# Attention and two dense layers on one core: the last batch passes layer one whole, and the weight conversion is divided anew

## The chip, the cores and the metric

The kernel runs on one core of a Trainium2 chip. The metric is the device time of one launch in microseconds (us). Engines are named as the profile names them: PE (matrix engine; PEld is its weight load), DVE (vector), ACT (scalar), POOL (GpSimd) and SP (the queue that issues all DMAs here).

## What is computed

Attention over 4 batches x 8 heads, 576 positions, head size 64, in which only scores within `tau` of the row's maximum count; then two dense layers over the 4 x 576 = 2304 tokens, each of width 512 with 2048 hidden units.

```python
scores = scale * (q @ k.T)
scores = where(scores >= max(scores) - tau, scores, -1e9)
attn = softmax(scores);  x = attn @ v
h = x @ w_in1;  g = where(h >= 1, h, where(h <= -1, 0, (h + 1)**2 / 4));  x = g @ w_out1
h = x @ w_in2;  g = h * clip(h + 3, 0, 6) / 6;                            out = g @ w_out2
```

The dense weights come as 64-bit numbers. Every product is made of three passes over split operands (high part x high, high x low, low x high).

## The kernel before

**Tokens.** The first 512 positions of a batch are a wide group; the last 64 of all four batches make one more group of 256 (the tail group). DRAM buffers `xd`, `x2p`, `x2d` hold the input of layer one, a partial output and the output of layer one, one buffer for each of the five groups.

**Hidden units** go in 16 blocks of 128, `f` = 0 to 15. A block of a group is `em_h` (line 520: 12 matmuls into a bank of PSUM, then the activation on DVE, ACT and DVE, lines 538 to 540, the split into `gh` on ACT, line 546, and `gl` on POOL, line 547), and later its share of the output (`em_part`, line 575, for narrow groups, `em_out`, line 556, for wide ones: 12 matmuls in all).

**Weights.** `split_a` and `split_b` (lines 107 and 129) turn one item (half of a block's weights, 128 x 512) into a high and a low part: ACT line 114, DVE lines 116, 119 (on POOL while the attention runs alone), 121 and 123, POOL line 125, ACT line 131, POOL line 133. There are 64 items, 32 for each layer. `Weights.half()` emits half an item; the callbacks `ahead1`, `ahead2`, `ahead3` say how many go ahead of each block. The loaded raw item lies in one of two buffers `w_raw`. Blocks 0 to 8 have fixed space (`wbase`), which layer two takes over when layer one has used it for the last time.

**Stages.** (1) Attention alone, with 18 items converted beside it. (2) From the first finished batch on, `dense1` (line 644) feeds narrow groups (256 tokens, 9 blocks of hidden units) of layer one into the attention: nine groups, the last of them the tail group; what is left of them runs behind the attention. Their sums go to `x2p`. (3) `dense` (line 668) takes the five wide groups through the other 7 blocks, reads `x2p` back (`load_part`), adds it (`fin_whole`, line 609) and stores `x2d`. (4) `dense` again: layer two, 16 blocks of each group, `fin_out`.

**Space.** The narrow groups' tiles lie in a pool `mt`. At the end of stage 2 it is closed and two pools, `mt2` and `g2` with the wide groups' `r`, `gh` and `gl`, are opened in the same place (lines 769 to 772), so their first writers wait for the last readers of `mt`, the stores to `x2p`.

**Order.** A scheduler of the framework places the instructions by its own plan of times within the dependencies; each engine then runs its list in that order. Every block's last ACT, DVE and POOL instruction is a pin (line 550) behind which the next conversion item is put.

Of the kernel before, what the change touches and what calls it, by code (L numbers as in the profile page):

```python
# [18 lines left out]
def kernel(  # L19
# [12 lines left out]
    nc = tc.nc  # L32
# [10 lines left out]
    NG = NT // GRP  # L43
# [3 lines left out]
    NF1 = 9  # L47
    NE = 1
# [4 lines left out]
    CSTEP = 2  # L53

# [34 lines left out]
    def load_w(kind, m, f):  # L89
        t = stage.tile([128, 512, 2], U32, tag="w_raw", name="w_raw", bufs=2)  # L90
# [48 lines left out]
    class Weights:  # L139
# [11 lines left out]
        def prefetch(self):  # L151
            while self.loaded < min(len(self.items), self.done + 2):
# [96 lines left out]
    def unit_qk(j, nm, h):  # L249
# [15 lines left out]
        else:  # L265
# [5 lines left out]
            T.transpose(tm[:, MAIN:SEQ], n[0:TAIL, 4, :], ident[0:TAIL, 0:TAIL])  # L271
# [224 lines left out]
    xsp = {"p": mt, "x": mt, "g": None, "bufs": 1, "xt": "io"}  # L496
    H_TAGS = ["Q2"]
    A_TAGS = ["P0", "P1"]

    def split_x(key):  # L500
        m, g, ph = key
        n = GRP if ph == 1 else WIDE[g]
        src = narrow(xd, g) if ph == 1 else (x2d if m == 1 else xd)[g]
        r = []
        for kk in range(KD):
            if kk % 2 == 0:
                t = xsp["x"].tile([128, 2, n], F32, tag=xsp["xt"], name="xst", bufs=2)
# [12 lines left out]
    def em_h(key, m, f):  # L520
# [14 lines left out]
        hp_, hb = (mt, HOLD) if key[2] == 1 else (xsp["g"], MLAG + 1)  # L535
# [108 lines left out]
    def dense1(ready, ahead):  # L644

        for n, l in enumerate(steps):
            if n < n_h:
                g, f = divmod(n, NF1)
                key = (0, g, 1)
                if key not in xs:  # L650
                    while not ready(g):
                        yield None
                    split_x(key)
                ahead(n, f)
                yield from em_h(key, 0, f)
                if f == NF1 - 1:
                    xs.pop(key)
                    if g + 1 < NG and ready(g + 1):
                        split_x((0, g + 1, 1))
                    if g + 1 == NG:  # L660
                        xsp.update(x=ctx.enter_context(tc.tile_pool(name="xs2", bufs=1)), xt="xst", bufs=2)
                        split_x((0, 0, 2))
                yield 0.33
# [4 lines left out]
    def dense(m, ph, groups, fs, fin, ahead, following):  # L668

        seq = [(g, f) for g in groups for f in fs]  # L670
        splits = [(m, g, ph) for g in groups] + following

        def out_block(n, i):
            g, f = seq[n]
            em_out((m, g, ph), m, f, f == fs[0], f == fs[-1], fin, i)
# [3 lines left out]
        for n, (g, f) in enumerate(seq):  # L679
# [3 lines left out]
            ahead(n, f)  # L683
            for c in em_h(key, m, f):
                pass
            if f == fs[-3] and m == 0:
                load_part(g)
            if f == fs[-2]:
                for nxt in splits[splits.index(key) + 1:][:1]:
                    split_x(nxt)  # L690
            if f == fs[-1]:
# [71 lines left out]
    wpool["p"] = ctx.enter_context(tc.tile_pool(name="wext", bufs=1))  # L763
# [4 lines left out]
    H_TAGS[:] = ["Q0", "Q1", "Q2", "Q3"]  # L768
    mt_es.close()
    xsp["p"] = ctx.enter_context(tc.tile_pool(name="mt2", bufs=1, side="right"))  # L770
    xsp["g"] = ctx.enter_context(tc.tile_pool(name="g2", bufs=1, side="right"))
    wpool["e"] = ctx.enter_context(tc.tile_pool(name="wmore", bufs=1, side="right"))

    def ahead2(n, f):
        k = n - (NW - 1) * len(fs2) - MLAG - 1
# [3 lines left out]
        if n < len(fs2):  # L779
            weights.upto(2 * KF - 2 * len(fs2) + 2 * n + 2)  # L780

    def ahead3(n, f):
# [36 lines left out]
```

## Time and profile before

| | us |
|---|---|
| median of 3 runs (lowest, highest) | 1255.71 (1251.21, 1258.08) |
| the profiled execution | 1253.57 |
| its span, first to last instruction | 1251.8 |
| PE busy | 1179.3 (94%) |
| DVE busy | 776.8 (62%) |
| POOL busy | 749.3 (60%) |
| ACT busy | 647.0 (52%) |

The shares are means over stages that differ. Matmuls overlap in the records (one of 512 columns is recorded with 0.39 us, the next begins earlier), so how fast PE works is read from the starts of matmuls, and how much it loses from its idle time and from the granted clock of a stretch.

### The profile page before, as it was taken

The page shows a single profiled execution, that of the slowest core. Times are in us where ns is not written, and L with a number is a line of the kernel's source. Part 1 is how long each engine was busy: PE and PEld are TensorE (multiplying, and loading weights), DVE is VectorE, ACT ScalarE, POOL GpSimd, SP SyncE. Part 2 cuts the span into 40 slices and gives each one's busy share as a digit, 9 for nine tenths or more (in the row PEclk, how much of TensorE's full clock was granted, in tenths as well). Part 3 has the DMA queues.
Part 4 walks back from the last instruction along what each step waited for, and adds up shares of the span by engine and source line. Part 5 has one row for each costly group of instructions (what it writes and reads, how often), then busy time and mean ns, then how long its engine had stood idle before and what let it go on. Part 6 is the DMA issues. An engine that isn't in the chain of part 4 may idle for free.

```text
span 1251.8 us, 19651 instructions
## 1 busy us (share of the span) xinstructions
PE 1179.3 (94%) x6964; PEld 1005.2 (80%) x6964; DVE 776.8 (62%) x1620; ACT 647.0 (52%) x1201; POOL 749.3 (60%) x749
## 2 busy tenths in 40 slices
PE   7889999899999999989998889998999999999998
PEld 5555579888988989989997677896888888888886
DVE  6988888888888888697728888468721121121111
ACT  5766667778787888665414344343432222232222
POOL 6999768889998999766616665336722222222221
PEclk9999999999999999989999899999999999999999
DMA  5444431122222211153313444334100010000000
GB/s 137 120 117 116 115 85 49 53 66 58 66 67 58 75 49 38 46 181 123 119 42 114 152 122 152 118 115 121 51 18 34 1 37 31 1 35 1 17 1 34
DMA packets 100881, 91.81 MB, mean 73 GB/s; under 512 B 51376, under 2 KB 85168, under 8 KB 100784
## 3 DMA queue, kind: packets, MB, share of 16 engines
q1 hardware_dynamic: 100784, 90.57, 24.4%
q8 instruction: 55, 0.90, 0.3%
q14 instruction: 42, 0.34, 0.1%
HBM read 71.66 MB, written 18.87 MB: 72 GB/s over the span
## 4 chain that ended last, share of the span: by engine, by line
PE 57%; DVE 16%; POOL 15%; issue 5%; DMA 3%; ACT 2%; SPq 1%; POOLq 0%; DVEq 0%; ACTq 0%
PE Q L529 22%; PE P L571 19%; PE Q L586 5%; POOL Gl L373 4%; PE P L311 3%; DVE w_c L116 2%; PE Q L348 2%; DVE p L327 2%; DVE w_c L119 2%; PE Q L403 2%; PE Q L401 2%; DVE w_c L121 2%; DMA w_raw<-in_moe_w_in_dram 2%; POOL Gh L374 2%; POOL w_c L119 2%
## 5 line engine op out<-in xcount | busy, mean ns | idle before, releaser
L547 POOL TENSOR_TENSOR gl<-r,gh 128x256 fp32r<-128x256 f32 (+1 forms) x196 | 207.8, 1061 | 366.5 <-ACT gh L546 327.6
L529 PE MATMUL Q<-xh,wih 128*128 128x256 f32 (+1 forms) x784 | 267.6, 343 | 10.0 <-DVE r L540 9.2
L529 PE MATMUL Q<-xl,wih 128*128 128x256 f32 (+1 forms) x784 | 264.3, 337 | 4.5 <-DVE xl L512 4.4
L529 PE MATMUL Q<-xh,wil 128*128 128x256 f32 (+1 forms) x784 | 263.5, 337 | 0.0
L543 DVE SCALAR_TENSOR_TENSOR r<-r,Q 128x512 f32<-128x512 f32 (+1 forms) x80 | 50.6, 634 | 265.3 <-ACT r L542 263.0
L529 PEld LDWEIGHTS Q<-xh,wih 128*128 128x128 f32 x784 | 150.2, 192 | 29.5 <-DVE r L540 11.3
L529 PEld LDWEIGHTS Q<-xl,wih 128*128 128x128 f32 x784 | 150.7, 192 | 20.6 <-DVE xl L512 5.3
L546 ACT ACTIVATE gh<-r 128x256 fp32r<-128x256 f32 (+1 forms) x196 | 100.9, 515 | 122.4 <-DVE r L543 45.4
L529 PEld LDWEIGHTS Q<-xh,wil 128*128 128x128 f32 x784 | 150.7, 192 | 14.9
L327 DVE SCALAR_TENSOR_TENSOR p<-p,th,e 128x576 f32<-128x576 f32 x144 | 149.4, 1041 | 13.6 <-ACT e L323 10.5
L373 POOL TENSOR_TENSOR Gl<-pf,Gh 128x512 fp32r<-128x512 f32 (+1 forms) x110 | 147.1, 1337 | 15.7 <-ACT Gh L372 10.3
L542 ACT ACTIVATE r<-Q,three 128x512 f32<-128x512 f32 (+1 forms) x80 | 51.5, 644 | 165.8 <-PE Q L529 161.3
L323 ACT ACTIVATE e<-p,nm 128x576 f32<-128x576 f32 x144 | 111.0, 771 | 34.0 <-DVE p L322 32.8
L539 ACT ACTIVATE r<-r,half 128x256 f32<-128x256 f32 (+1 forms) x116 | 64.2, 557 | 117.5 <-DVE r L538 117.3
L125 POOL TENSOR_TENSOR w_c<-w_c,w_raw 128x512 int32<-128x512 int32 x64 | 90.0, 1407 | 57.1 <-DVE w_c L123 36.4
L571 PE MATMUL P<-woh,gh 128*128 128x512 f32 x288 | 113.3, 395 | 6.0 <-DVE ob L611 3.3
L322 DVE TENSOR_SCALAR_CACHE_REDUCE p<-P 128x576 f32<-128x576 f32 x144 | 107.4, 747 | 18.0 <-PE P L298 10.6
L311 PE MATMUL P<-kst,qh 128*128 128x288 f32 x320 | 99.5, 326 | 16.3 <-DVE xu L444 6.3
L571 PE MATMUL P<-wol,gh 128*128 128x512 f32 x288 | 113.2, 393 | 0.0
L571 PE MATMUL P<-woh,gl 128*128 128x512 f32 x288 | 111.9, 393 | 0.0
L586 PE MATMUL Q<-gh,woh 128*128 128x256 f32 x324 | 97.3, 300 | 0.7 <-DVE ob L597 0.5
L586 PE MATMUL Q<-gl,woh 128*128 128x256 f32 x324 | 92.5, 285 | 1.2 <-POOL gl L547 1.1
(102 smaller groups left out, 2739.9 us busy)
## 6 DMA issues: line engine op xcount, KB each, us to landing
w_raw<-in_moe_w_in_dram SPq DMA_DIRECT2D x32, 512.0 KB, 3.9
w_raw<-in_moe_w_out_dram SPq DMA_DIRECT2D x32, 512.0 KB, 3.7
qn<-in_q_dram SPq DMA_DIRECT2D x32, 256.0 KB, 3.6
xst<-xd SPq DMA_DIRECT2D x20, 256.0 KB, 3.2
x2p<-ob SPq DMA_DIRECT2D x18, 256.0 KB, 2.4
kn<-in_k_dram SPq DMA_DIRECT2D x32, 128.0 KB, 2.2
xd<-xu SPq DMA_DIRECT2D x16, 256.0 KB, 2.3
xst<-xd SPq DMA_DIRECT2D x8, 512.0 KB, 3.9
```

The costliest lines, as they stand in the source:

```text
L125: x = G.tensor_tensor(out=c.bitcast(I32), in0=c.bitcast(I32), in1=r, op=ALU.add)
L311: mm = T.matmul(s[:, e, 0:HS], l, r[:, e * HS:(e + 1) * HS], start=(x == 0), stop=(x == len(ops) - 1))
L322: V.tensor_scalar(out=p, in0=s, scalar1=-1.0, scalar2=3e38, op0=ALU.mult, op1=ALU.min, accum_out=nm)
L323: S.activation(out=e, in_=p, func=ACTF.Exp, bias=nm, scale=-1.0)
L327: V.scalar_tensor_tensor(out=p, in0=p, scalar=th, in1=e, op0=ALU.is_le, op1=ALU.mult, accum_out=zt[j][:, i:i + 1])
L373: G.tensor_tensor(out=lo[:, :, d], in0=f[:, 0:4, b], in1=f32(hi[:, 0:4, d]), op=ALU.subtract)
L529: mm = T.matmul(h, l[:, kk * 128:(kk + 1) * 128], r, start=(x == 0), stop=(x == 3 * KD - 1))
L539: S.activation(out=r, in_=r, func=ACTF.Square, scale=0.5, bias=half)
L546: x = S.activation(out=gh, in_=r, func=ACTF.Copy)
L547: y = G.tensor_tensor(out=gl, in0=r, in1=f32(gh), op=ALU.subtract)
L571: T.matmul(a, l, r, start=(first and x == 0), stop=(last and x == 2))
L586: mm = T.matmul(o, l, r, start=(f == 0 and x == 0 and i == 0), stop=(f == NF1 - 1 and x == 2 and i == 1), skip_group_check=True)
```

## The change

- **Narrow groups** cover batches 0, 1 and 2 alone (six groups instead of nine), with ten blocks of hidden units instead of nine. Twenty items of weights are converted before and beside the attention instead of eighteen.
- **Batch 3 and the tail group** pass layer one in one piece behind the narrow groups, all 16 blocks, without `x2p`; batches 0 to 2 follow with the 6 blocks that are left. Layer two's order is batch 3, 0, 1, the tail, batch 2.
- **The switch.** A pool `g1` of its own holds the wide groups' tiles for the first four wide blocks; the second halves of the last narrow group's sums (`behind`) are emitted behind those blocks' first matmuls; `mt` is closed after them.
- **Layer two's weights** wait for the tail group to use a block for the last time (`n_free`), so their conversion begins some blocks into the tail group; a third `w_raw` buffer is added.
- **The conversion behind the attention**: the sign bit is taken off by ACT (`Abs`) instead of DVE; line 119's clamp stays on DVE. During the attention the mask is on DVE and the clamp on POOL, now also beside hosted blocks.
- `split_x` loads a wide group in four pieces through three buffers instead of two pieces through two. Sums that need no `x2p` go out by ACT and DVE in turn. A transpose of 64 rows of K becomes one of 128.

```diff
-    NG = NT // GRP
+    NG = (NB - 1) * MAIN // GRP
-    NF1 = 9
-    NE = 1
+    NF1 = 10
+    RAW = 3
...
-        x = V.tensor_scalar(
-            out=c, in0=t[:, :, 1], scalar1=0x7FFFFFFF, scalar2=None, op0=ALU.bitwise_and)
-        after(x, pins["V"])
-        (V if mode["mlp"] else G).tensor_scalar(
-            out=f32(c), in0=f32(c), scalar1=2.0 ** -15, scalar2=122879.9921875, op0=ALU.max, op1=ALU.min)
+        if mode["att"]:
+            x = V.tensor_scalar(
+                out=c, in0=t[:, :, 1], scalar1=0x7FFFFFFF, scalar2=None, op0=ALU.bitwise_and)
+            G.tensor_scalar(
+                out=f32(c), in0=f32(c), scalar1=122879.9921875, scalar2=2.0 ** -15, op0=ALU.min, op1=ALU.max)
+        else:
+            S.activation(out=f32(c), in_=f32(t[:, :, 1]), func=ACTF.Abs)
+            x = V.tensor_scalar(
+                out=f32(c), in0=f32(c), scalar1=2.0 ** -15, scalar2=122879.9921875, op0=ALU.max, op1=ALU.min)
+            after(x, pins["V"])
...
-            T.transpose(tm[:, MAIN:SEQ], n[0:TAIL, 4, :], ident[0:TAIL, 0:TAIL])
+            T.transpose(tm[:, MAIN:MAIN + 128], n[:, 4, :], ident)
...
+                src = pool.tile([128, n], F32, tag="xst", name="xst", bufs=3)
+                nc.sync.dma_start(out=src, in_=(x2d if m == 1 else xd)[g][:, kk, :])
...
+            if n == n_h - 3 and not mode["att"]:
+                split_x((0, NB - 1, 2))
...
+    def behind():
+        for l in steps[n_h:]:
+            for g, half, f in l:
+                for _ in em_part((0, g, 1), half, f):
+                    pass
+                yield
...
+    NLATE = 2
+    early = ctx.enter_context(tc.tile_pool(name="wext", bufs=1))
+    for f in range(NF1, KF - NLATE):
+        wpool[f] = early
+    wide["x"] = ctx.enter_context(tc.tile_pool(name="xs2", bufs=1))
+    g_es = ExitStack()
+    wide["g"] = g_es.enter_context(tc.tile_pool(name="g1", bufs=1))
...
+    seq2 = [(g, f) for g in (NB - 1, NB) for f in range(KF)]
+    n_free = len(seq2) - KF + MLAG + 1
+    seq2 += [(g, f) for g in range(NB - 1) for f in fs2]
+    n_last = len(seq2) - len(fs2) + MLAG + 1
+    left = behind()
+    SWITCH = MLAG + 2
+    def rest(n):
+        if n <= MLAG:
+            for _ in range(100 if n == MLAG else 4):
+                if next(left, 0) == 0:
+                    break
+        if n == MLAG:
+            H_TAGS[:] = ["Q0", "Q1", "Q2", "Q3"]
+            mt_es.close()
+            wide["p"] = ctx.enter_context(tc.tile_pool(name="mt2", bufs=1, side="right"))
+            wide["g2"] = ctx.enter_context(tc.tile_pool(name="g2", bufs=1, side="right"))
+    def ahead2(n, g, f):
...
+        limit = 2 * KF if n > SWITCH + MLAG else 2 * (KF - NLATE)
+        limit += 2 * max(0, min(n - n_free, NF1)) + 2 * max(0, n - n_last)
         for _ in range(2):
-            if weights.done < 2 * KF + 2 * NF1 + 2 * NE + max(0, 2 * (k - NE)):
+            if weights.done < limit:
                 weights.half()
...
-    order2, order3 = list(range(NW)), list(range(NW - 2)) + [NW - 1, NW - 2]
+    order3 = [NB - 1, *range(NB - 2), NB, NB - 2]
```

**DVE just behind the attention.** `xl` is the low part of a split input (128x512 of a wide group, 128x256 of a narrow one or the tail), `w_c` a weight item in conversion, `r` a block's activation. Before:

```order
L116 TENSOR_SCALAR w_c_7568<-w_raw_7469 128x512
L119 TENSOR_SCALAR w_c_7568<-w_c_7568 128x512
L121 TENSOR_SCALAR w_c_7568<-w_c_7568 128x512
L538 TENSOR_SCALAR r_7588<-Q1_7575 128x256
L123 SCALAR_TENSOR_TENSOR w_c_7568<-w_raw_7469,w_c_7568 128x512
L512 TENSOR_TENSOR xl_8906<-xst_8903,xh_8905 128x512
L512 TENSOR_TENSOR xl_8910<-xst_8903,xh_8909 128x512
L540 TENSOR_TENSOR r_7588<-Q1_7575,r_7588 128x256
L512 TENSOR_TENSOR xl_8916<-xst_8913,xh_8915 128x512
L538 TENSOR_SCALAR r_7625<-Q2_7612 128x256
```

Now:

```order
L125 TENSOR_SCALAR w_c_7572<-w_c_7572 128x512
L522 TENSOR_TENSOR xl_7984<-xst_7981,xh_7983 128x512
L128 TENSOR_SCALAR w_c_7572<-w_c_7572 128x512
L548 TENSOR_SCALAR r_7592<-Q1_7579 128x256
L130 SCALAR_TENSOR_TENSOR w_c_7572<-w_raw_7487,w_c_7572 128x512
L522 TENSOR_TENSOR xl_7990<-xst_7987,xh_7989 128x512
L522 TENSOR_TENSOR xl_7640<-xst_7637,xh_7639 128x256
L522 TENSOR_TENSOR xl_7996<-xst_7993,xh_7995 128x512
L548 TENSOR_SCALAR r_7629<-Q2_7616 128x256
L522 TENSOR_TENSOR xl_7644<-xst_7637,xh_7643 128x256
```

The mask has gone from the item's head; the last narrow group's own split (`xl_7640` to `xl_7654`) now stands behind one item and two wide pieces; before, three items and eight wide pieces stood ahead of the next narrow group's split.

**DVE at the switch from narrow to wide blocks.** The first `r` of 128x512 is the first wide block's. Before:

```order
L123 SCALAR_TENSOR_TENSOR w_c_9014<-w_raw_8539,w_c_9014 128x512
L597 COPY ob_8941<-Q3_8800 128x512
L538 TENSOR_SCALAR r_9038<-Q2_9025 128x512
L538 TENSOR_SCALAR r_9072<-Q3_9059 128x512
L540 TENSOR_TENSOR r_9038<-Q2_9025,r_9038 128x512
L116 TENSOR_SCALAR w_c_9048<-w_raw_8626 128x512
L540 TENSOR_TENSOR r_9072<-Q3_9059,r_9072 128x512
L116 TENSOR_SCALAR w_c_9082<-w_raw_9023 128x512
L119 TENSOR_SCALAR w_c_9048<-w_c_9048 128x512
```

Now:

```order
L130 SCALAR_TENSOR_TENSOR w_c_8092<-w_raw_7875,w_c_8092 128x512
L548 TENSOR_SCALAR r_8116<-Q1_8103 128x512
L550 TENSOR_TENSOR r_8116<-Q1_8103,r_8116 128x512
L548 TENSOR_SCALAR r_8165<-Q2_8152 128x512
L607 COPY ob_8136<-Q3_7907 128x512
L550 TENSOR_TENSOR r_8165<-Q2_8152,r_8165 128x512
L548 TENSOR_SCALAR r_8210<-Q0_8197 128x512
L550 TENSOR_TENSOR r_8210<-Q0_8197,r_8210 128x512
L548 TENSOR_SCALAR r_8279<-Q0_8266 128x512
```

Before, the copy of a narrow sum (`ob`) stands ahead of the first wide `r`, and two items follow at once; now the first wide block is finished ahead of that copy, and no item follows until seven wide blocks have passed.

**DVE where layer two's weights are converted beside wide or tail blocks.** Before, in the first wide group (lines 538 and 540 are a block's activation):

```order
L116 TENSOR_SCALAR w_c_9130<-w_raw_9057 128x512
L119 TENSOR_SCALAR w_c_9130<-w_c_9130 128x512
L121 TENSOR_SCALAR w_c_9130<-w_c_9130 128x512
L538 TENSOR_SCALAR r_9200<-Q2_9187 128x512
L123 SCALAR_TENSOR_TENSOR w_c_9130<-w_raw_9057,w_c_9130 128x512
L116 TENSOR_SCALAR w_c_9176<-w_raw_9091 128x512
L540 TENSOR_TENSOR r_9200<-Q2_9187,r_9200 128x512
L119 TENSOR_SCALAR w_c_9176<-w_c_9176 128x512
L538 TENSOR_SCALAR r_9254<-Q3_9241 128x512
L121 TENSOR_SCALAR w_c_9176<-w_c_9176 128x512
```

Now, in the tail group (lines 548 and 550 are the activation, 125, 128 and 130 the item):

```order
L125 TENSOR_SCALAR w_c_8923<-w_c_8923 128x512
L128 TENSOR_SCALAR w_c_8923<-w_c_8923 128x512
L130 SCALAR_TENSOR_TENSOR w_c_8923<-w_raw_8459,w_c_8923 128x512
L548 TENSOR_SCALAR r_8947<-Q1_8934 128x256
L550 TENSOR_TENSOR r_8947<-Q1_8934,r_8947 128x256
L125 TENSOR_SCALAR w_c_8969<-w_c_8969 128x512
L128 TENSOR_SCALAR w_c_8969<-w_c_8969 128x512
L130 SCALAR_TENSOR_TENSOR w_c_8969<-w_raw_8505,w_c_8969 128x512
L548 TENSOR_SCALAR r_8993<-Q2_8980 128x256
L550 TENSOR_TENSOR r_8993<-Q2_8980,r_8993 128x256
L548 TENSOR_SCALAR r_9039<-Q3_9026 128x256
```

An item has three DVE instructions instead of four, and the blocks it stands between have 256 columns instead of 512.

## Rows read from the trace of the kernel before

**Rows 1.** stretches: start:end, us, busy PE PEld DVE ACT POOL (count), PEclk, DMA share, GB/s

```profile
0.00:175.00 175.00, 153.50 (x795) 98.45 (x796) 145.05 (x315) 114.52 (x239) 140.38 (x141) 0.96 0.45 122
175.00:525.00 350.00, 330.79 (x2588) 312.46 (x2587) 298.51 (x812) 275.11 (x503) 315.77 (x365) 1.00 0.20 55
525.00:656.00 131.00, 124.37 (x959) 120.55 (x959) 88.62 (x159) 59.21 (x129) 69.45 (x66) 0.97 0.35 113
656.00:780.00 124.00, 109.13 (x443) 86.44 (x442) 106.09 (x135) 51.25 (x87) 75.91 (x55) 0.94 0.45 138
780.00:848.00 68.00, 68.00 (x372) 59.20 (x371) 37.40 (x59) 27.30 (x49) 24.15 (x23) 1.00 0.35 109
848.00:900.00 52.00, 46.58 (x200) 37.71 (x199) 44.14 (x51) 21.37 (x36) 38.57 (x29) 0.93 0.34 101
900.00:1250.00 350.00, 346.91 (x1619) 290.36 (x1617) 57.04 (x92) 98.22 (x164) 85.02 (x73) 1.00 0.06 19
```

**Rows 2.** waits of PE after 525 us: who waited for whom, us, times, longest

```profile
PE P L571 <- DVE ob L611: 11.6, 7, 3.8
PE Q L529 <- DVE r L540: 4.7, 3, 3.4
PE Q L529 <- DVE xl L512: 4.4, 3, 3.0
PE P L571 <- ACT gh L546: 3.7, 2, 2.1
```

**Rows 3.** timeline of DVE at 659 us: start, length, instruction, idle before it

```profile
659.79 1.29 DVE L538 TENSOR_SCALAR r<-Q 128x512 f32<-128x512 f32 x2 [13.61 <-DMA x2p<-ob]
```

**Rows 4.** timeline of PE, eleven matmuls of 256 columns in a row, first and last

```profile
521.02 0.28 PE L529 MATMUL Q<-xh,wil 128*128 128x256 f32 x1
...
522.21 0.28 PE L586 MATMUL Q<-gh,woh 128*128 128x256 f32 x1
```

**Rows 5.** timeline of PE, eleven matmuls of 512 columns in a row, first and last

```profile
899.71 0.39 PE L571 MATMUL P<-wol,gh 128*128 128x512 f32 x1
...
901.98 0.39 PE L571 MATMUL P<-woh,gl 128*128 128x512 f32 x1
```

**Rows 6.** groups by line and form, whole span: busy us, mean ns, idle before

```profile
L125 POOL TENSOR_TENSOR w_c<-w_c,w_raw 128x512 int32<-128x512 int32 x64 | 90.0, 1407 | 57.1 <-DVE w_c L123 36.4 <-issue 11.0 <-ACT r L539 4.9
...
L123 DVE SCALAR_TENSOR_TENSOR w_c<-w_raw,w_c 128x512 uint32<-128x512 uint32 x64 | 54.9, 860 | 1.1
...
L121 DVE TENSOR_SCALAR w_c<-w_c 128x512 uint32<-128x512 uint32 x64 | 51.8, 811 | 8.1 <-POOL w_c L119 6.7
...
L119 DVE TENSOR_SCALAR w_c<-w_c 128x512 f32<-128x512 f32 x46 | 44.0, 959 | 1.1
...
L114 ACT ACTIVATE w_raw<-w_raw 128x512 int32<-128x512 uint32 x64 | 43.1, 673 | 41.5 <-DMA w_raw<-in_moe_w_in_dram 19.6 <-DMA w_raw<-in_moe_w_out_dram 17.6 <-DVE w_c L121 2.6
...
L119 POOL TENSOR_SCALAR w_c<-w_c 128x512 f32<-128x512 f32 x18 | 38.5, 2137 | 3.9 <-DVE w_c L116 2.8
L540 DVE TENSOR_TENSOR r<-Q,r 128x256 f32<-128x256 f32 x88 | 36.4, 415 | 14.5 <-ACT r L539 14.2
...
L540 DVE TENSOR_TENSOR r<-Q,r 128x512 f32<-128x512 f32 x28 | 19.2, 687 | 10.2 <-ACT r L539 10.2
```

**Rows 7.** single lines on DVE from 656 to 780 us: ns min/median/max

```profile
L116 DVE TENSOR_SCALAR w_c<-w_raw x19: 414/1314/1529, 661.9 to 775.4; 128x512 uint32<-128x512 uint32 x19
...
L119 DVE TENSOR_SCALAR w_c<-w_c x19: 414/1390/1498, 664.2 to 776.9; 128x512 f32<-128x512 f32 x19
...
L121 DVE TENSOR_SCALAR w_c<-w_c x19: 409/427/1423, 666.0 to 777.4; 128x512 uint32<-128x512 uint32 x19
...
L123 DVE SCALAR_TENSOR_TENSOR w_c<-w_raw,w_c x19: 675/693/1176, 667.2 to 777.8; 128x512 uint32<-128x512 uint32 x19
...
L512 DVE TENSOR_TENSOR xl<-xst,xh x11: 678/1471/1778, 681.3 to 773.9; 128x512 fp32r<-128x512 f32 x8, 128x256 fp32r<-128x256 f32 x3
```

More of the change, by code (lines that the diff above doesn't have):

```diff
@@ L108, in split_a @@
         t = wraw.pop((kind, m, f))
-        pool = wbase if f < NF1 else wpool["e"] if m == 1 and f < NF1 + NE else wpool["p"]
+        pool = wbase if f < NF1 else wpool[f]
         hi = pool.tile([128, 512], F32R, tag=f"w{kind}h{f}", name=f"w{kind}h{f}")
@@ L151, in prefetch @@
         def prefetch(self):
-            while self.loaded < min(len(self.items), self.done + 2):
+            while self.loaded < min(len(self.items), self.done + RAW):
                 load_w(*self.items[self.loaded])
@@ L534, in em_h @@
                 yield 0.33
-        hp_, hb = (mt, HOLD) if key[2] == 1 else (xsp["g"], MLAG + 1)
+        hp_, hb = (mt, HOLD) if key[2] == 1 else (wide["g"], MLAG + 1)
         r = hp_.tile([128, n], F32, tag="r", name="r", bufs=2)
@@ L644, in dense1 @@
     def dense1(ready, ahead):
[L646 to L663, printed above, removed]
+        for n, l in enumerate(steps[:n_h]):
+            g, f = divmod(n, NF1)
+            key = (0, g, 1)
+            if key not in xs:
+                while not ready(g):
+                    yield None
+                split_x(key)
+            ahead(n, f)
+            yield from em_h(key, 0, f)
+            if f == NF1 - 1:
+                xs.pop(key)
+                if g + 1 < NG and ready(g + 1):
+                    split_x((0, g + 1, 1))
+            if n == n_h - 3 and not mode["att"]:
+                split_x((0, NB - 1, 2))
+            yield 0.33
             for g, half, f in l:
@@ L666, in dense1, with dense @@
                 yield 0.33
-    def dense(m, ph, groups, fs, fin, ahead, following):
-        seq = [(g, f) for g in groups for f in fs]
-        splits = [(m, g, ph) for g in groups] + following
+    def behind():
[4 more added lines that the diff above has]
+                yield
+    def dense(m, ph, seq, fin, ahead, following, rest=None):
+        fs = {}
+        for g, f in seq:
+            fs.setdefault(g, []).append(f)
+        splits = [(m, g, ph) for g in fs] + following
         def out_block(n, i):
             g, f = seq[n]
-            em_out((m, g, ph), m, f, f == fs[0], f == fs[-1], fin, i)
+            em_out((m, g, ph), m, f, f == fs[g][0], f == fs[g][-1], fin, i)
             if i == blocks(m, g) - 1:
@@ L682, in dense @@
                 split_x(key)
-            ahead(n, f)
+            ahead(n, g, f)
             for c in em_h(key, m, f):
                 pass
-            if f == fs[-3] and m == 0:
+            if rest is not None:
+                rest(n)
+            if m == 0 and g < NB - 1 and f == fs[g][-3]:
                 load_part(g)
-            if f == fs[-2]:
+            if f == fs[g][-2]:
                 for nxt in splits[splits.index(key) + 1:][:1]:
                     split_x(nxt)
-            if f == fs[-1]:
+            if f == fs[g][-1]:
                 xs.pop(key)
@@ L767, with ahead3 @@
         pass
[L768 to L775, printed above, removed]
+    seq2 = [(g, f) for g in (NB - 1, NB) for f in range(KF)]
[15 more added lines that the diff above has]
+    def ahead2(n, g, f):
+        if n == SWITCH:
+            wide["g"] = wide["g2"]
+        if n == SWITCH + MLAG + 1:
+            g_es.close()
+            late = ctx.enter_context(tc.tile_pool(name="wlate", bufs=1))
+            for x in range(KF - NLATE, KF):
+                wpool[x] = late
+        limit = 2 * KF if n > SWITCH + MLAG else 2 * (KF - NLATE)
+        limit += 2 * max(0, min(n - n_free, NF1)) + 2 * max(0, n - n_last)
         for _ in range(2):
-            if weights.done < 2 * KF + 2 * NF1 + 2 * NE + max(0, 2 * (k - NE)):
+            if weights.done < limit:
                 weights.half()
-        if n < len(fs2):
-            weights.upto(2 * KF - 2 * len(fs2) + 2 * n + 2)
-    def ahead3(n, f):
+        if g == NB - 1:
+            weights.upto(2 * f + 2)
+    def ahead3(n, g, f):
         for _ in range(4):
```

45 lines of the change are left out of this document (24 added, 21 removed).

## The prediction

> **What bounds the kernel now.** I read first the busy time of the engines in seven stretches. Attention ends at about 525 us, the rest of the narrow blocks at 656, layer one's wide groups at about 848, and the last weight item is converted before 900. The reader should compare a stretch's PE time with its length, and its granted clock (the column behind POOL's) with 1.00. From 780 to 848 and from 900 on PE hardly loses anything [rows 1]: there the time is matmuls and nothing else, and the change leaves their columns alone. What can be gained lies in three stretches: 525 to 656, 656 to 780 and 848 to 900. PE stands idle in them for 6.6, 14.9 and 5.4 us, and the lower clock takes (1 - 0.97) x 131 = 3.9, (1 - 0.94) x 124 = 7.4 and (1 - 0.93) x 52 = 3.6 us more [rows 1]. That is 10.5, 22.3 and 9.0 us, 41.8 in all.
>
> The waits of PE say who is late: results copied out by DVE before a bank of PSUM can be used again (11.6 us), activations and split inputs on DVE (4.7 and 4.4), `gh` on ACT (3.7) [rows 2]. These are mostly DVE's, which is busy for 106 of 124 us in the worst stretch and does weight items there [rows 1]. One wait has another cause: at the switch DVE sat idle for 13.6 us until a store to `x2p` had landed [rows 3], since the wide groups' tiles lie where the narrow ones' were; PE waited 3.4 us for that activation, the longest in its line [rows 2]. With the clock's fall behind it I put the switch at 5.8 us.
>
> In attention PE, DVE and POOL are busy 331, 299 and 316 of 350 us [rows 1]; three engines near their limits, and a change of matmul shapes moves little there.
>
> **The change part by part.**
>
> *Shapes.* 288 matmuls of 256 columns become 144 of 512. Eleven in a row start within 1.19 us, so one of 256 takes 0.119 [rows 4]; one of 512 takes 0.227 [rows 5]. 288 x 0.119 - 144 x 0.227 = **-1.6 us**.
>
> *Attention.* Two more items are converted there, and the order puts them ahead of the 48th of 144 score blocks, at the end of the first stretch. Each costs POOL 2.14 + 1.41 us and one more pass like the latter [rows 6], together 9.9. POOL is busy 140 of the first 175 us [rows 1], so I cost them at 0; if that cover is gone, 9.9. The transposes of K over 128 rows: 32 of them, no row shows the difference; a whole narrow matmul each, 3.8 us, bounds it on either side, and I take 0, as they stand among waits. The narrow blocks hosted in the attention are as many as before (42).
>
> *525 us on (10.5 us lost before).* About 17 narrow blocks are left instead of 39, with 8 items instead of 14. The loss here sat at the start, where splits queued behind items (4.4 us [rows 2] and a fall of the clock). The order has fewer of both ahead of the narrow split, but the pieces of batch 3 and of the tail still come in the same few us. I take half, **5**; ends 2 and 10.
>
> *The switch (5.8).* The first four wide blocks no longer write where `mt` lies, and the last narrow group's second sums, 60 matmuls or 7 us, stand on PE behind the first wide matmuls and cover the first activations. The stores to `x2p` then have more than a block to land before the fifth wide block writes into that space. I take **1.5**; ends 0 and 5.8.
>
> *Layer two's items beside the tail and batches 0 and 1 (16.5 before, beside wide blocks).* This is the term that decides. The order puts 20 items beside 12 tail blocks and some 10 wide ones. PE needs 12 x 24 x 0.119 + 10 x 24 x 0.227 = 34.3 + 54.5 = 88.8 us. DVE needs for an item 0.96 + 0.81 + 0.86 = 2.63 us, for a block two operations of 0.415 or of 0.687 (the first counted like the second) [rows 6], and eight wide split pieces at 1.47 [rows 7]: 52.6 + 10.0 + 13.7 + 11.8 = 88.1. So DVE is just as full as PE. At 656 to 780 us it was DVE 106 against about 102 of PE at full clock [rows 1], and the part without the switch lost 16.5 us, 16%. At a slightly better ratio I take 15% of 88.8: **13 us**; ends 0 (all fits) and 22 (the whole stretch's 22.3 of 102 [rows 1]). ACT gets one operation more for each item, like the 0.67 us of line 114 [rows 6]; POOL has 2 x 1.41 an item; both stay below PE's time.
>
> The sum is not the whole, for lines 116, 119 and 121 take 0.41 us at best and about 1.4 at worst, with little between [rows 7]: they wait inside, and what waits once can wait again in the next instruction (a rival below). The Trainium skill (SBUF — State Buffer, the section on the ports) says that DVE operations in a 2-port mode or with two SBUF inputs share a port pair with GpSimd as an exclusive lock, and that the loser stands for the other's whole instruction. The two values of these rows agree with that; the time that would follow is the rival's 1252 in place of 1236.
>
> *The other boundaries.* Three groups are added to `x2p` instead of five, at some 1.7 us of wait each (11.6 in 7 [rows 2]), with less on DVE: **2**; ends 0 and 5. *Layer two's start (9.0).* Ten items instead of twelve, at 2.63 us instead of four operations: **4**; ends 1 and 9. The third load buffer takes pressure from SP; the queue's new risk is a fourth input piece that waits for a free buffer with weight loads behind it, which three loaded items cover.
>
> *Sum.* 5 + 1.5 + 13 + 2 + 4 = 25.5 instead of 41.8: -16.3. With the shapes -17.9. From the profiled execution's 1253.6 that gives 1235.7; I forecast **1236**. The median of the runs stands 2.1 above that execution, less than they differ among themselves.
>
> **The rivals.** *The spread works throughout* (22%): DVE's queue stays short, and the losses are 2 + 0 + 3 + 1 + 2 = 8. For it speaks that the tail's sums need no addition and leave by two engines; against it that DVE, POOL and ACT are all nearly full there. 1253.6 - 41.8 + 8 - 1.6 = **1218**, or 1214 with the transposes.
>
> *The mask's wait passes to the clamp behind it* (12%). Line 116's median of 1.31 us is 0.9 above its bare 0.41 [rows 7]; if line 119 now meets the POOL operation that the mask met, an item spares DVE only the bare time. 20 x 0.9 = 18 us more make DVE's sum 106 against 88.8, an excess of 17; from 656 to 780 us the excess was 4 (106 against 102) and the loss 16.5, so some 12 come on top: 29 instead of 13, **1252**. By the Trainium skill's rule of the lock, named above, this is what happens. Against it: an item's next DVE operations often stand behind a POOL operation that has ended by then, as line 121's median of 0.43 shows [rows 7].
>
> *The extra items aren't hidden in the attention* (8%): 9.9 us more, **1246**. For it speaks POOL's 90% from 175 us on [rows 1].
>
> *Slower: POOL and DVE block each other in the tail* (8%). A tail block gives PE only 24 x 0.119 = 2.86 us, and one item on POOL alone takes 2.8. If every line meets a busy POOL, an item costs DVE 1.50 + 1.42 + 1.18 = 4.10 and a split piece 1.78 [rows 7]: 82 + 23.7 + 14.2 = 119.9 against 88.8, a loss of 31, and as many falls of the clock as from 656 to 780, 7.4 [rows 1]; with layer two's start at its old 9.0 the losses are 5 + 1.5 + 38.5 + 2 + 9 = 56, and the time 1253.6 + 14.2 - 1.6 = **1266**. It is slower than before from the point at which the stretch loses 31 instead of 13. Against it: from 848 to 900 POOL was busy 39 of 52 us and DVE 44 [rows 1], and PE lost 17%, not a third.
>
> **How the numbers follow.** The forecast's case has 50%, from 1225 to 1244. The range of 1214 to 1256 takes in the spread, the attention's items and the passed wait, and leaves out the slower case and the lowest ends. 0.5% is 6.3 us, about what a measurement can tell from no change: below 1247 (of the profiled execution's time) lie the forecast, the spread and a part of the attention's and the mask's cases, 0.78; within it 0.14; slower 0.08.
>
> **What would show it.** Right: from the end of attention to the switch one dip of the clock at most; no idle DVE behind a store to `x2p`; in batch 3 a full PE; then one stretch of some 90 us in which DVE is busy over 85% and PE loses about 15%; layer two from its sixth block on as before. Wrong, on the good side: that stretch shows PE without gaps; on the bad side: the clamp's median near 1.4 us and PE waiting for DVE in every tail block, or POOL's waits in the attention grown.

## The result and the profile of the changed kernel

The changed kernel takes **1219.3 us** (median of 4 runs, 1218.2 to 1220.5), the kernel before 1256.6 beside it: a ratio of 0.971, 95% interval 0.968 to 0.974. The forecast was 1236, the range 1214 to 1256; direction and range held, and the gain was twice the one forecast. The profiled execution took 1220.3 us, its span 1218.5. One run of e3 below, its profiled one, took 1614.5 us at a granted clock of 0.66, so e3 stands for its other three runs and its profile isn't used.

Where the time came from is read by cutting the span at one instruction that both kernels have, the last of the 144 score blocks on DVE (line 322 before, 329 now; most lines move by 7 to 11). Timeline of DVE in the kernel before (start, length, instruction):

```profile
510.16 0.75 DVE L322 TENSOR_SCALAR_CACHE_REDUCE p<-P 128x576 f32<-128x576 f32 x1
```

and in the changed kernel:

```profile
493.91 0.75 DVE L329 TENSOR_SCALAR_CACHE_REDUCE p<-P 128x576 f32<-128x576 f32 x1
```

Up to there 16.3 us were gained, in the part whose change I had costed at nothing. Behind it the span was 1251.8 - 510.2 = 741.6 and is 1218.5 - 493.9 = 724.6: **17.0 us**, where the prediction's sum said 17.9.

Stretches of the changed kernel (columns as in [rows 1]):

```profile
0.00:150.00 150.00, 133.43 (x730) 89.85 (x731) 131.69 (x283) 106.78 (x221) 109.84 (x135) 0.98 0.48 137
...
510.00:558.00 48.00, 44.65 (x335) 43.14 (x334) 36.48 (x64) 28.29 (x62) 30.48 (x27) 0.93 0.41 129
558.00:685.00 127.00, 127.00 (x718) 111.86 (x717) 54.74 (x90) 52.75 (x91) 53.88 (x46) 1.00 0.23 70
685.00:770.00 85.00, 75.36 (x367) 62.04 (x366) 71.76 (x95) 51.25 (x90) 62.42 (x47) 0.96 0.50 150
...
829.00:870.00 41.00, 36.46 (x152) 29.10 (x151) 23.14 (x29) 21.12 (x36) 31.21 (x24) 0.96 0.28 84
```

Counted as in the prediction (idle time of PE plus what the clock takes), the loss is 3.4 + 3.4 = 6.7 us behind the attention, 0 around the switch and in batch 3, 9.6 + 3.4 = 13.0 where layer two's items stand, 4.5 + 1.6 = 6.2 at layer two's start: 25.9 in place of 41.8. PE's waits after 520 us (who waited for whom: us, times, longest), which answer to [rows 2]:

```profile
PE P L581 <- DVE ob L622: 6.2, 3, 3.7
PE P L581 <- ACT gh L556: 4.9, 4, 2.2
PE P L581 <- DVE ob L626: 2.4, 1, 2.4
PE Q L539 <- DVE xl L522: 1.4, 2, 1.1
```

DVE is still late most often: `ob` behind it went from 11.6 to 8.6 us, and the waits for `r` and for the store at the switch [rows 3] are all but gone. The waits for `gh`, which ACT makes of DVE's `r`, grew from 3.7 to 4.9. The group of the clamp on POOL answers to line 119 in [rows 6], where it took 2137 ns:

```profile
L121 POOL TENSOR_SCALAR w_c<-w_c 128x512 f32<-128x512 f32 x20 | 15.5, 777 | 3.4 <-DVE w_c L119 2.8
```

Shape, type and constants are the same; the diff has only exchanged the two operations, minimum first and maximum second. The prediction never looked at that.

### The profile page after: what moved, and what is told of

The parts are those of the page before. It is cut to its first block, busy times and chain, and to the rows that moved or that the text cites. A ratio compares the mean times of both kernels' runs of the same rounds, so it can differ in the third digit from the quotient of the medians.

```text
span 1218.5 us, 19295 instructions
## 1 busy us (share of the span) xinstructions
PE 1160.1 (95%) x6820; PEld 992.8 (81%) x6820; DVE 715.1 (59%) x1543; ACT 667.1 (55%) x1222; POOL 724.7 (59%) x745
## 5 line engine op out<-in xcount | busy, mean ns | idle before, releaser
L557 POOL TENSOR_TENSOR gl<-r,gh 128x512 fp32r<-128x512 f32 (+1 forms) x190 | 205.0, 1080 | 380.9 <-ACT gh L556 365.8
L539 PE MATMUL Q<-xh,wih 128*128 128x512 f32 (+1 forms) x760 | 262.3, 345 | 0.9 <-ACT xh L521 0.7
L539 PE MATMUL Q<-xl,wih 128*128 128x512 f32 (+1 forms) x760 | 259.5, 341 | 1.4 <-DVE xl L522 1.4
L539 PE MATMUL Q<-xh,wil 128*128 128x512 f32 (+1 forms) x760 | 258.8, 341 | 0.0
L539 PEld LDWEIGHTS Q<-xh,wih 128*128 128x128 f32 x760 | 145.7, 192 | 19.3 <-ACT xh L521 1.4
L539 PEld LDWEIGHTS Q<-xl,wih 128*128 128x128 f32 x760 | 145.7, 192 | 18.4 <-DVE xl L522 1.9
L539 PEld LDWEIGHTS Q<-xh,wil 128*128 128x128 f32 x760 | 145.7, 192 | 15.7
L556 ACT ACTIVATE gh<-r 128x512 fp32r<-128x512 f32 (+1 forms) x190 | 99.3, 523 | 101.9 <-PE P L581 40.1
L318 PE MATMUL P<-kst,qh 128*128 128x288 f32 x320 | 99.3, 326 | 14.6 <-DVE xu L451 5.4
L318 PE MATMUL P<-kst,ql 128*128 128x288 f32 x320 | 91.6, 302 | 0.3 <-DVE ql L271 0.3
L355 PE MATMUL Q<-ident,p 128*128 128x128 f32 x576 | 88.4, 276 | 1.8 <-ACT pf L376 1.3
```

Of the source, the lines that this page charges most:

```text
L318: mm = T.matmul(s[:, e, 0:HS], l, r[:, e * HS:(e + 1) * HS], start=(x == 0), stop=(x == len(ops) - 1))
L355: x = T.transpose(tm[:, cc * 128:(cc + 1) * 128], p[:, cc * 128:(cc + 1) * 128], ident)
L539: mm = T.matmul(h, l[:, kk * 128:(kk + 1) * 128], r, start=(x == 0), stop=(x == 3 * KD - 1))
L556: x = S.activation(out=gh, in_=r, func=ACTF.Copy)
L557: y = G.tensor_tensor(out=gl, in0=r, in1=f32(gh), op=ALU.subtract)
```

## The experiments

Every kernel but e10 was run four times, beside four or seven runs of the kernel before; the median is of these runs, the last two columns are of the one that was profiled. "Behind" is its span minus the start of the last score block.

| kernel | median us | ratio, 95% interval | last score block | behind |
|---|---|---|---|---|
| before | 1254 to 1257 | | 510.2 | 741.6 |
| after | 1219.3 | 0.971 [0.968, 0.974] | 493.9 | 724.6 |
| e1: before, clamp min first | 1241.0 | 0.988 [0.986, 0.991] | 499.8 | 738.1 |
| e2: after, clamp max first | 1228.1 | 0.978 [0.975, 0.980] | 502.4 | 724.5 |
| e3: after, 64-row transpose | 1221.5 | 0.974 [0.971, 0.977] | | |
| e5: after, two raw buffers | 1225.2 | 0.976 [0.973, 0.979] | 497.8 | 725.1 |
| e6: e1, 128-row transpose | 1237.7 | 0.986 [0.984, 0.988] | 498.0 | 738.9 |
| e7: after, mask on DVE | 1232.2 | 0.981 [0.979, 0.983] | 499.6 | 732.0 |
| e8: after, old switch | 1223.7 | 0.976 [0.974, 0.979] | 498.9 | 728.7 |
| e9: after, all clamps on POOL | 1201.6 | 0.958 [0.956, 0.959] | 496.3 | 703.3 |
| e10: after, 30 probes | 1219.5 | (one run) | 493.6 | 723.8 |
| e11: e9, all masks on ACT | 1202.5 | 0.959 [0.957, 0.960] | 496.2 | 705.2 |
| e12: before, all clamps on POOL | 1214.3 | 0.969 [0.966, 0.972] | 495.4 | 716.0 |
| e13: e9, half of the small `Gh` on DVE | 1216.2 | 0.970 [0.968, 0.973] | 504.6 | 707.0 |

A warning from the table: e8 and e10 have the changed kernel's order on every engine up to the last score block, and in their profiles that block starts at 498.9 and 493.6. So 5 us there, in single profiles, tell nothing. The time of e8's profiled run was 1229.4 us, that of its other three 1223.4 to 1223.8.

### e1 and e2: the clamp alone, both ways

```diff
# e1, on the kernel before, for POOL's clamp only (in effect; the code picks the pair by `mode`)
-  scalar1=2.0 ** -15, scalar2=122879.9921875, op0=ALU.max, op1=ALU.min
+  scalar1=122879.9921875, scalar2=2.0 ** -15, op0=ALU.min, op1=ALU.max
# e2, on the changed kernel: the reverse
```

> The kernel before with one edit: POOL's clamp of the 18 items that are converted while attention runs alone takes the minimum first and the maximum second, as in the changed kernel; the order of the instructions on every engine stays word for word the same. Theory A (the gain in the attention comes from this clamp, 0.78 us in the changed kernel's trace against 2.14 before): POOL gives back 18 x 1.36 = 24 us, the last score block starts 8 to 14 us earlier, and the time is 1242 to 1249. Rival B (the gain there comes from the transposes of K, the third load buffer and the new place of the items): the clamp may be shorter, the time stays within 3 us of 1256. Rival C (the clamp's time doesn't hang on the order of its two operations but on what runs beside it): the clamp still takes about 2.1 us.

> The changed kernel with the clamp's two operations on POOL put back in the old order (maximum first), 20 items, nothing else moved on any engine. Theory A: the clamp takes 2.1 us again, POOL loses 20 x 1.36 = 27 us in the first stretch, the end of attention comes 10 to 16 us later and the time is 1229 to 1236. Rival B: within 4 us of 1219. Rival C: the clamp stays at 0.8 us.

The order of instructions is the same on every engine in both pairs, so only the clamp's time differs. e1 gave 13.6 us (1254.6 to 1241.0) and e2 cost 8.8, the fastest run of e2 (1224.5) being 4 us slower than the slowest of the changed kernel (1220.5): theory A, with 1 us more than its numbers in e1 and 1 less in e2. Within the profiles the last score block moves by 10.4 and 8.5 us. The clamp's group in e1 and then in e2:

```profile
L119 POOL TENSOR_SCALAR w_c<-w_c 128x512 f32<-128x512 f32 x18 | 13.9, 771 | 4.6 <-DVE w_c L116 3.5
```

```profile
L121 POOL TENSOR_SCALAR w_c<-w_c 128x512 f32<-128x512 f32 x20 | 41.1, 2059 | 2.9 <-DVE w_c L119 2.4
```

The first 150 us of e2, beside the first row of stretches above:

```profile
0.00:150.00 150.00, 130.46 (x693) 86.37 (x693) 128.54 (x267) 102.26 (x212) 129.05 (x132) 0.94 0.45 126
```

POOL is busier by 19 us and still has 21 us free, and yet fewer matmuls are done in the same time. POOL's free time is no cover, for others wait for the item's pieces on POOL while it is free elsewhere. In the kernel before this stood in [rows 6]: line 121 on DVE waited 6.7 us for the clamp on POOL; in e1 that wait no longer appears. From the changed kernel to e2 it is ACT (line 138) that waits longer in the first 150 us, 6.6 us in place of 2.4, for POOL's next operation on the item (line 132):

```profile
ACT wih L138 <- POOL w_c L132: 4.4, 3, 1.5
ACT woh L138 <- POOL w_c L132: 2.2, 3, 0.9
```

PE stands 3.0 us longer there (19.5 against 16.6) and its granted clock is 0.94 in place of 0.98, some 6 us more. The part of the clock may not be the clamp's: in e8, with the fast clamp and the same order there, it is 0.95. How these waits come down to PE was not followed.

### e10: the clamp by itself

```diff
+  p = stage.tile([128, 512], F32, tag="w_c", name="probe" + "ABCDEF"[n % 6], bufs=2)
+  x = G.tensor_scalar(out=p, in0=f32(wsp["i", 1, 0][0]), **PROBES[n % 6])
```

> The changed kernel with 30 more instructions on POOL in layer two, where POOL is a quarter busy: one behind each of 30 blocks, over the same 128x512 f32 tile of weights, in six kinds, five of each: A minimum then maximum with the kernel's constants, B maximum then minimum with the same, C the maximum alone, D the minimum alone, E and F as A and B with bounds of +-0.01. Their results are used by nobody. If what counts is which operation comes first: A, E and D about 0.6 us, B, F and C about 1.9. If it is the pairing of the two: C and D alike, B and F slow. If it is the data or the constants: E and F differ from A and B, and B is not slow on these weights. The time is that of the changed kernel within 3 us.

Single lines on POOL in e10, ns min/median/max, for A and B, C and D, E and F:

```profile
L845 POOL TENSOR_SCALAR probeA<-wih x5: 614/617/619, 944.7 to 1076.5; 128x512 f32<-128x512 f32 x5
L845 POOL TENSOR_SCALAR probeB<-wih x5: 1913/1919/1941, 950.1 to 1078.1; 128x512 f32<-128x512 f32 x5
L845 POOL TENSOR_SCALAR probeC<-wih x5: 1488/1492/1509, 955.5 to 1082.3; 128x512 f32<-128x512 f32 x5
L845 POOL TENSOR_SCALAR probeD<-wih x5: 1492/1493/1499, 960.9 to 1089.9; 128x512 f32<-128x512 f32 x5
L845 POOL TENSOR_SCALAR probeE<-wih x5: 615/617/618, 966.4 to 1092.0; 128x512 f32<-128x512 f32 x5
L845 POOL TENSOR_SCALAR probeF<-wih x5: 1928/1929/1930, 971.8 to 1093.3; 128x512 f32<-128x512 f32 x5
```

It is the pair: minimum followed by maximum takes 0.62 us, the other order 1.92, and either operation alone 1.49, more than the fast pair. The second pair of bounds changes nothing. The expectation that a single minimum would be fast fell. The Trainium skill (GPSIMD Engine Reference, section "Engine selection") says that GpSimd runs operations with one input at roughly line rate; A and E against B to D show that here it depends on the operations.

### e3, e5, e6: the transposes of K and the third raw buffer

```diff
# e3 on the changed kernel (e6 the reverse, on e1)
-  T.transpose(tm[:, MAIN:MAIN + 128], n[:, 4, :], ident)
+  T.transpose(tm[:, MAIN:SEQ], n[0:TAIL, 4, :], ident[0:TAIL, 0:TAIL])
# e5
-  RAW = 3
+  RAW = 2
```

> The changed kernel with the last transpose of K over 64 rows again, as before; the scheduler, which plans by its own times, moves some instructions with it. In the trace of before the matmul behind a transpose of 64 rows started 0.09 us later than behind one of 128 rows, 32 times: theory D (that is on the path) gives 3 us, 1222. Rival B, as far as it rests on the transposes, 5 us or more. If the transposes stand among waits, within 1.5 us of 1219.

> The changed kernel with two raw load buffers and two items loaded ahead instead of three; the scheduler moves many instructions with it. In the trace of before ACT's line 114 waited 17.6 us for raw loads in the first 175 us, in the changed kernel 7.9. Rival B, as far as it rests on the buffer: 5 to 10 us slower, 1224 to 1230, with the difference in the first 175 us. Theory A: the raw loads' wait is covered, within 4 us of 1219.

> The kernel before with POOL's clamp in the new order (as in e1) and, on top, the last transpose of K over 128 rows; the scheduler moves some instructions with it. e1 ended its last score block at 499.8 us, the changed kernel at 493.9. Theory D (the 5.9 us that the clamp leaves over are mainly the transposes): last score block at 494 to 497 us, time 1235 to 1239. Rival H (they come from how items and hosted blocks stand in the attention): last score block at 499 to 502, time 1240 to 1244.

e3 is 2 to 3 us above the changed kernel by its times and its ratio, e6 3 below e1, with overlapping intervals: a few us at most for the transposes, not settled. e5 is 6 us slower, its last score block 3.9 later and the rest the same to 0.5; but the scheduler reordered hundreds of instructions with it, and 3.9 us lies within what e8 and e10 differ by. So of the 16.3 us in the attention 8.5 (e2) to 10.4 (e1) are the clamp's by the profiles, for nothing else differs in those pairs; the 6 to 8 that are left, partly the spread of single profiles, are open.

### e7 and e8: the mask on DVE, and the old switch

```diff
# e7
-  S.activation(out=f32(c), in_=f32(t[:, :, 1]), func=ACTF.Abs)
+  x = V.tensor_scalar(out=c, in0=t[:, :, 1], scalar1=0x7FFFFFFF, scalar2=None, op0=ALU.bitwise_and)
# e8: all of behind() runs, mt is closed and mt2, g2 are opened ahead of the first wide block
+  for _ in left:
+      pass
...
+  wide["g"] = wide["g2"]
+  rest = None
```

> The changed kernel with the sign bit taken off by DVE again (mask) behind the attention instead of by ACT; clamp and all else as they are. 44 items, 16 of them between 685 and 770 us, get a DVE instruction of 0.41 us at best, 1.31 as the kernel before showed. Theory S (DVE is what these stretches hang on, and sharing its work out is what counts): from the last score block to the end 724.6 us become 732 to 742, most of it between 685 and 770 us, time 1227 to 1237. Rival N (what counts there is where the items stand, not who does them): within 4 us of 1219.

> The changed kernel with the switch as it was: all sums of the last narrow group stand ahead of the first wide block, and the first wide blocks' r, gh and gl lie where mt was. All that goes before is in the same order on every engine. My prediction priced the old switch at 5.8 us and the new one at 1.5: 4.3 us slower, 1223 to 1225, with DVE idle behind a store to x2p near 560 us and the clock low behind it. Rival: in the changed kernel no items stand around the switch, so the copies and stores come at once: within 1.5 us of 1219 or up to 3 slower.

e7: 13 us slower, 7.4 of it behind the attention, so theory S at the lower end of its numbers (732.0 of 732 to 742); the other 5.6 lie before the last score block, where its order also differs, and are not told apart from the spread there. From 685 to 770 us DVE is now busy 81 of 85 us and PE stands for 11.4 instead of 9.6, at a lower clock. That is 4.3 us more loss here, of 8.0 in all stretches behind the attention:

```profile
685.00:770.00 85.00, 73.63 (x369) 60.54 (x368) 80.75 (x106) 39.82 (x73) 62.73 (x49) 0.93 0.45 135
```

e8: 4.4 us slower by time, 4.1 behind the last score block, where the prediction said 5.8 - 1.5 = 4.3. DVE again sits idle until a store to `x2p` has landed, as in [rows 3] (timeline, idle before it in brackets):

```profile
583.12 1.29 DVE L548 TENSOR_SCALAR r<-Q 128x512 f32<-128x512 f32 x2 [12.05 <-DMA x2p<-ob]
```

### e9 and e12: every clamp on POOL, in the fast order

```diff
# e9, on the changed kernel, behind the attention too
-  x = V.tensor_scalar(
-      out=f32(c), in0=f32(c), scalar1=2.0 ** -15, scalar2=122879.9921875, op0=ALU.max, op1=ALU.min)
-  after(x, pins["V"])
+  x = G.tensor_scalar(
+      out=f32(c), in0=f32(c), scalar1=122879.9921875, scalar2=2.0 ** -15, op0=ALU.min, op1=ALU.max)
+  after(x, pins["G"])
# e12, on the kernel before: all 64 clamps so, nothing else
```

> The changed kernel with the clamp on POOL (minimum first) behind the attention too, so that DVE has two instructions for an item instead of three. In the changed kernel from 685 to 770 us DVE is busy 71.8 and POOL 62.4 of 85 us; 16 items would move 16 x 0.96 = 15 us from DVE and give POOL 16 x 0.61 to 0.78 = 10 to 12. Theory S: DVE is what is late, the stretch loses less, 1213 to 1217. Rival P: POOL becomes the late one there (75 of 85 us) and the chain of an item is longer by a hand-over: 1220 to 1230.

> The kernel before with the clamp of every item on POOL, minimum first; nothing of the change's new order, pools or sharing with ACT. Behind the attention DVE loses 46 x 0.96 = 44 us of work. e1 (the first 18 items alone) gave 1241.0. Theory S (the losses behind the attention are DVE's queue): 8 to 16 of the 41.8 us lost there come back, 1225 to 1233. Rival O (they come from the order: items, splits and sums standing together, and the switch): 1237 to 1243. What is left to e9's 1201.6 is then the new order's part.

e9 is **1201.6 us**, faster than both kernels, and beyond theory S's range. Its stretches:

```profile
510.00:558.00 48.00, 45.47 (x351) 44.15 (x350) 30.29 (x58) 27.78 (x62) 29.83 (x31) 0.96 0.40 124
685.00:770.00 85.00, 84.57 (x431) 72.09 (x430) 57.94 (x78) 49.42 (x90) 65.28 (x57) 1.00 0.49 151
770.00:829.00 59.00, 57.35 (x249) 46.18 (x248) 38.03 (x47) 32.51 (x54) 46.10 (x40) 1.00 0.51 162
829.00:870.00 41.00, 41.00 (x182) 33.94 (x182) 16.27 (x20) 19.24 (x33) 33.54 (x29) 1.00 0.16 47
```

Where items stand beside batches PE now loses 0.4 + 1.7 us instead of 13, at layer two's start nothing, and the clock stays up. Counted as before, 6.5 us are lost behind the attention in place of 25.9. Idle time of PE and a fall of the clock went together, and with the idle time both are gone (0.4 us idle at a clock of 1.00 from 685 to 770 us, against 9.6 at 0.96): 21 us behind the attention for 44 x 0.93 = 41 us of DVE's work (mean of line 125 on DVE from 685 to 770 us). On POOL the clamp keeps its price by the median while DVE works beside it (the mean is 0.68 us):

```profile
L125 POOL TENSOR_SCALAR w_c<-w_c x44: 603/617/1058, 158.0 to 857.5; 128x512 f32<-128x512 f32 x44
```

The Trainium skill (Perfetto Trace Analysis, "Optimizing Scalar/DVE Operations") warns that moving work between DVE and GpSimd might not help, since they share an SBUF port. Here it helped by 17.7 us.

e12 is the bigger surprise: the kernel before, with one call changed, takes 1214.3, below theory S's 1225 to 1233 and no slower than the changed kernel (whose 1219.3 comes from another series of runs; the intervals of the two ratios overlap). In its stretch that answers to 656 to 780 us of [rows 1] DVE is busy 92 us instead of 106, and PE loses 4.1 + 1.2 instead of 22.3:

```profile
641.00:765.00 124.00, 119.86 (x521) 98.39 (x520) 92.19 (x125) 57.97 (x96) 94.89 (x77) 0.99 0.46 144
```

With the clamp in place the rest of the change (order, pools, the mask on ACT, the third load buffer) is still worth 1214.3 - 1201.6 = 12.7 us, with intervals well apart.

### e11 and e13: what the attention hangs on

```diff
# e11, on e9: the first 20 items as the others
-  x = V.tensor_scalar(out=c, in0=t[:, :, 1], scalar1=0x7FFFFFFF, scalar2=None, op0=ALU.bitwise_and)
+  S.activation(out=f32(c), in_=f32(t[:, :, 1]), func=ACTF.Abs)
# e13, on e9: line 381
-  G.tensor_tensor(out=hi[64:128, 4, d], ...
+  (V if mode["n"] % 2 else G).tensor_tensor(out=hi[64:128, 4, d], ...
```

> As e9 (clamp on POOL, minimum first, everywhere; 1201.6), and the sign bit of the first 20 items taken off by ACT too, not by DVE. In the first 150 us of the changed kernel DVE is busy 131.7, ACT 106.8 and POOL 109.8 us: if DVE is what the first stretch hangs on, 20 x 0.44 = 9 us less on DVE bring the 36th score block 3 to 8 us earlier and the time to 1194 to 1199; if PE's own chain (scores, exponentials, transposes) sets it, or ACT's 13 us more delay the exponentials, 1201 to 1206.

> As e9 (clamp on POOL, minimum first, everywhere; 1201.6, last score block at 496.3), and every second of the small subtractions of line 381 (64x128, mean 0.69 us on POOL, 106 of them from 150 to 500 us) goes to DVE, where an instruction of that size takes 0.2 to 0.3 us. In e9 POOL is busy 320 and DVE 306 of those 350 us, and DVE waits 18.6 us for these subtractions. Theory Q (what the attention hangs on is POOL's queue): POOL gets back some 37 us for 10 to 15 on DVE, the last score block starts 5 to 15 us earlier, 1187 to 1197. Rival R (DVE is as full, or PE's own chain sets it): last score block at 495 to 500, 1200 to 1206.

e11 changes nothing (1202.5): DVE has 11 us less to do in the first 150 us and nothing starts earlier. e13 is 14.6 us slower: rival R, and worse than it said. From 150 to 500 us, e9 and then e13:

```profile
150.00:500.00 350.00, 327.27 (x2558) 307.50 (x2557) 305.69 (x837) 277.09 (x504) 320.37 (x367) 1.00 0.22 60
```

```profile
150.00:500.00 350.00, 322.14 (x2494) 302.81 (x2494) 327.71 (x868) 272.63 (x495) 290.53 (x308) 0.99 0.22 59
```

POOL has 30 us less, DVE 22 more, and PE falls behind by 64 matmuls. The moved instructions take a median of 0.6 us on DVE, not the 0.2 to 0.3 I had counted on (line 381 in e13, ns min/median/max, then the 64x128 form alone with busy us and mean ns, on DVE in e13 and on POOL in e9):

```profile
L381 DVE TENSOR_TENSOR Gh<-pf,Gh x51: 219/605/1395, 169.5 to 496.8; 64x128 fp32r<-64x128 f32 x41, 64x64 fp32r<-64x64 f32 x10
L381 DVE TENSOR_TENSOR Gh<-pf,Gh 64x128 fp32r<-64x128 f32 x41 | 28.2, 687 | 1.6 <-ACT Gh L379 0.3
L381 POOL TENSOR_TENSOR Gh<-pf,Gh 64x128 fp32r<-64x128 f32 x84 | 57.8, 689 | 6.6
```

So beside the hosted blocks DVE is the worse place for these subtractions, though POOL is the busier engine: one of 64x128 takes 0.69 us in the mean on either (on POOL in e9, the third row). From e11, the mask isn't what is late in the first stretch. What sets the first stretch was not found.

## Why the prediction was half right

**The step that failed is "Attention".** "Each costs POOL 2.14 + 1.41 us" took the clamp's price from a row of the other order; it was 0.78. And "POOL is busy 140 of the first 175 us, so I cost them at 0" took free time of an engine for cover, and so left out what a shorter instruction on POOL can give back. With the old order the changed kernel is 8.8 us slower (e2), and the swap alone makes the kernel before 13.6 faster (e1). A part that a diff rewrites without moving it, here two names in a call, is an edit with a price of its own; I had listed it under what stays.

**Behind the attention the sum stood, in part by luck.** In us, with the forecast first: behind the attention 5, measured 6.7; the switch 1.5, measured 0 (and e8 gave the difference from the old one as 4.1 to 4.4 for 4.3); items beside the tail and the batches, with the boundaries, 13 + 2, measured 13.0; layer two's start 4, measured 6.2. Sum 25.5 against 25.9, but four terms were off by 1.5 to 2.2 us, two up and two down, and these errors cancel. The term that decides gave the right loss, 15% of its stretch, but with DVE less full than the working had it: 71.8 of 85 us, not 88.1 of 88.8. There 7.5 us of DVE's idle time end with the mask on ACT (line 124, in the rows of line 125 below), a hand-over that the prediction did not price. The -1.6 for the shapes has no run of its own.

**The rivals.** "The spread works throughout" named 1218, and the time came out there, but not by its mechanism: it wanted a loss of 3 us where items stand, and 13.0 was measured. The right time is no evidence for it; e9 is what that rival looks like. "The mask's wait passes to the clamp" is the rival that needs care. By medians it did not come: the clamp's is 0.96 us on DVE from 685 to 770 us, where line 119's was 1.39 [rows 7]. But these durations spread widely, from 0.4 to 1.5 us, and busy time goes by means. Groups with busy us, mean ns and idle time before, from 656 to 780 us in the kernel before:

```profile
L119 DVE TENSOR_SCALAR w_c<-w_c 128x512 f32<-128x512 f32 x19 | 20.3, 1071 | 0.5
L116 DVE TENSOR_SCALAR w_c<-w_raw 128x512 uint32<-128x512 uint32 x19 | 19.3, 1018 | 6.2 <-DMA w_raw<-in_moe_w_out_dram 3.7 <-DMA w_raw<-in_moe_w_in_dram 1.8 <-POOL wol L133 0.7
L123 DVE SCALAR_TENSOR_TENSOR w_c<-w_raw,w_c 128x512 uint32<-128x512 uint32 x19 | 14.0, 739 | 0.4
...
L121 DVE TENSOR_SCALAR w_c<-w_c 128x512 uint32<-128x512 uint32 x19 | 11.5, 609 | 0.4
```

From 685 to 770 us in the changed kernel, and then in e7, where the mask is back on DVE (line 124):

```profile
L130 DVE SCALAR_TENSOR_TENSOR w_c<-w_raw,w_c 128x512 uint32<-128x512 uint32 x16 | 16.8, 1051 | 0.4
L125 DVE TENSOR_SCALAR w_c<-w_c 128x512 f32<-128x512 f32 x15 | 13.9, 925 | 7.6 <-ACT w_c L124 7.5
L128 DVE TENSOR_SCALAR w_c<-w_c 128x512 uint32<-128x512 uint32 x16 | 13.5, 845 | 0.3
```

```profile
L130 DVE SCALAR_TENSOR_TENSOR w_c<-w_raw,w_c 128x512 uint32<-128x512 uint32 x16 | 17.8, 1110 | 0.3
L127 DVE TENSOR_SCALAR w_c<-w_c 128x512 f32<-128x512 f32 x16 | 16.8, 1048 | 0.2
L128 DVE TENSOR_SCALAR w_c<-w_c 128x512 uint32<-128x512 uint32 x16 | 14.1, 882 | 0.4
L124 DVE TENSOR_SCALAR w_c<-w_raw 128x512 uint32<-128x512 uint32 x15 | 12.5, 835 | 1.0 <-POOL wol L140 1.0
```

An item took 3.44 us of DVE before and takes 2.82 now, in place of the prediction's 2.63. So 0.62 us were spared: more than the bare 0.41 that this rival left, less than line 116's whole 1.02, since the lines of the last two steps (121 and 123, now 128 and 130) are longer by 0.24 and 0.31. The wait passed in part, though not to the clamp. The two stretches have different blocks beside the items, however. e7 is the closer pair, with the mask back and, but for the order that the scheduler made of it, all else as now: from 685 to 770 us an item takes 3.88 there, so the mask's going spared 1.06 us, and no line behind it grew. "The extra items aren't hidden" and the slower case fell too: even with the old, slow clamp (e2) the last score block starts at 502.4 us, not later than the 510.2 of before, and no stretch behind the attention lost 31 us.

**What the prediction did not ask** is which engine should have the clamp. It read that DVE was what was late, took 2.14 us for granted as POOL's price and so never saw that, at 0.62 (0.68 in e9's mean), POOL was the place for it.

## What to carry to other kernels

When a diff rewrites an instruction without moving it, price the new form by itself; if no row of the trace shows that form, its bounds reach from the cheapest to the dearest row of the same shape on that engine, in both directions. An engine that is free for a fifth of a stretch need not hide what others wait for within a chain. Where one engine is late in several stretches, look first for the single operation that another engine does as cheaply: one call of that kind (e12, the clamp's order and engine: 39.6 us) was worth more here than all the rest of the change (e2, which has the old order of the clamp: 26.6 us).

## What the runs showed of the hardware

GpSimd's pair of minimum then maximum over 128x512 f32 takes 0.62 us, maximum then minimum 1.92, and either alone 1.49 (e10); the pairs were measured with two sets of bounds and took the same with both. Why is not shown. And a subtraction of 64x128 takes 0.28 us on DVE at best, but 0.69 in the mean in a stretch where POOL is busy 83% of the time (e13): a minimum in a trace is not the price that a full stretch will pay. That POOL is the cause of the longer ones is not shown by a run.
